# First layer norms of the last three row blocks moved to ScalarE, with statistics from summed outputs, in a fused attention and GLU kernel

## The chip, the cores and the metric

The kernel runs on one core of one Trainium2 chip. The core has a matrix engine (TensorE, PE in the profile; PEld is its weight load), a vector engine (VectorE, DVE), a scalar engine (ScalarE, ACT), a general engine (GpSimd, POOL) and a sync engine (SP), which here only issues DMAs. Each engine takes its instructions in the order in which they stand in its queue and waits on semaphores for the others. The metric is the device time of one execution in microseconds (us); less is better.

## The reference

One sequence of 2048 rows of width 576, two sublayers in fp32, each behind a layer norm without weights and with a residual:

```python
h  = x + attention(layernorm(x)) @ wo      # 32 heads of 18, each row attends to itself and
                                           # 7 earlier rows, 2 apart (sliding, dilated)
h2 = h + (sigmoid(n @ w_gate) * (n @ w_up)) @ w_down     # n = layernorm(h), width 4608

def layernorm(x, eps=1e-5):
    m, v = mean(x), var(x)
    return (x - m) / sqrt(v + eps)
```

The change concerns `layernorm(x)`, the first norm.

## The kernel before, in words

Rows are split into even and odd ones (attention steps by two rows), and each of these into two halves: four blocks of 512 rows, `BLOCKS` (0,0), (0,1), (1,0), (1,1), called 0 to 3. A block has four row tiles of 128 rows (`NS`), j = 0 to 3.

**First stage, up to about 223 us.** For each block `ln1` (line 338) takes the rows `xb`, normalises tile by tile into `xn` (`ln_j`, line 118; the last 64 columns are stored twice so that the contraction is a multiple of 128), transposes on TensorE (`tr_main`, line 137, four 128x128 transposes into a PSUM bank `mm`; `tr_rest`, line 142, one into a bank `acc`), and splits the result into a high and a low part for fp32r matmuls: `split` (line 103: ScalarE copies to the high part, VectorE subtracts for the low one) and `split_rest` (line 107, the same for the last chunk, with `th` as its output). In the profile `th` and `tl` are these parts, L104 and L105 the two halves of `split`, L108 and L109 those of `split_rest`, and `tok` is the tile behind `xn`.

`qkv` (line 377) then multiplies: for each block and each of four head groups four passes of `tok_major` (line 146) of 14 matmuls 128x432 into a bank `acc`, each evicted by ScalarE (line 384) into `ev`; after the fourth, three DMAs issued from ScalarE's queue (lines 388 and 390) write q, k and v to DRAM scratch. There are 64 such passes. `attention` (line 161) reads them back through SP (`q`, `kw`, `vw`) and is VectorE work (products, reductions, softmax, lines 182 to 219) but for one Exp on ScalarE (line 196). The generators are interleaved in the source: `norm_under` (line 424) normalises block b while passes of an earlier block are issued: block 1 under group 1 of block 0, block 2 under group 0 of block 1, block 3 under group 0 of block 2.

Four attentions of block 0 fill its output; then `front` (line 478) transposes it, projects it with `wo`, adds the residual, normalises again (`proj_j`, line 240, which calls `ln_j` too), and writes the operand to DRAM (line 505, `x<-tok` in the profile).

**Second stage.** The 4608 hidden columns of the MLP in chunks of 128, TensorE matmuls with 512 rows as the moving side (lines 609 to 616 and 723), with weights loaded and split by ScalarE and VectorE (L104 and L105, `w`, `wg`, `d`). The attention that is left, of blocks 1 to 3, and their projections run beside it. Blocks 2 and 3 share a scheme with fewer multiplications (`down_seven`, L785 to L794).

**What sets the order.** A scheduler places each engine's instructions in a fixed order when the kernel is built, from the order of the source and from priorities (`tc.high_priority`; `HI` is 400). Nothing is reordered while it runs. The first norm's priority is `2 * HI` for block 0, 0 for block 1 and `HI` for blocks 2 and 3 (line 345).

**The norm itself.** In `ln_j` VectorE takes mean and variance (two `bn_stats` over 288 columns, `bn_aggr`, an addition of eps), GpSimd raises to -1/2. For blocks 0 and 1 VectorE then subtracts and scales in one pass and copies the last 64 columns (lines 134 and 135). For blocks 2 and 3 (`on_act`) VectorE negates the mean (line 129) and ScalarE makes two passes, centring with a bias and scaling, and the small copy (lines 130 to 132).

Of the kernel before, what the change touches and what calls it, by code (L numbers as in the profile page):

```python
# [15 lines left out]
F32 = mybir.dt.float32  # L16
F32R = mybir.dt.float32r
AF = mybir.ActivationFunctionType
ALU = mybir.AluOpType
AX = mybir.AxisListType  # L20

P = 128
S = 2048
D = 576
# [6 lines left out]
NS = 4  # L31
TB = P * NS
DM = 512
DR = D - DM
DX = D + DR
# [5 lines left out]
EPS = 1e-5  # L41
# [11 lines left out]
HI = 400  # L53
# [7 lines left out]
def kernel(ctx, tc, x, wqkv, wo, wmlp, out):  # L61
    nc = tc.nc
    dve, act, pool, pe, sp = nc.vector, nc.scalar, nc.gpsimd, nc.tensor, nc.sync
# [9 lines left out]
    sm = ctx.enter_context(tc.tile_pool(name="sm", bufs=2))  # L73
# [12 lines left out]
    mhalf = cst.tile([P, 1], F32, name="mhalf")  # L86
# [16 lines left out]
    def split(hi, lo, src):  # L103
        act.activation(hi, src, AF.Copy)  # L104
        splits.append(dve.tensor_tensor(lo, src, f32(hi), ALU.subtract))  # L105

    def split_rest(t, src):
        act.activation(t, src, AF.Copy)  # L108
        dve.tensor_tensor(t[64:128], src[64:128], f32(t[64:128]), ALU.subtract)  # L109
# [5 lines left out]
                sp.dma_start(bass.AP(tensor=a.tensor, offset=a.offset,  # L115
                                     ap=[[LP * CG // 16, 16], [1, LP * CG // 16]]), zero)

    def ln_j(xj, xn, on_act):
        bs = sm.tile([P, 2, 6], F32, bufs=4, name="bs")
        mv = sm.tile([P, 2], F32, bufs=4, name="mv")  # L120
        rstd = sm.tile([P, 1], F32, bufs=4, name="rstd")
        for k in range(2):
            dve.bn_stats(bs[:, k], xj[:, k * DH2:(k + 1) * DH2])
        dve.bn_aggr(mv, bs)
        dve.tensor_scalar(rstd, mv[:, 1:2], EPS, None, ALU.add)
        pool.tensor_tensor(rstd, rstd, mhalf, ALU.pow)
        if on_act:
            nm = sm.tile([P, 1], F32, bufs=4, name="nm")
            dve.tensor_scalar(nm, mv[:, 0:1], -1.0, None, ALU.mult)
            act.activation(xn[:, :D], xj, AF.Identity, bias=nm)  # L130
            act.activation(xn[:, :D], xn[:, :D], AF.Copy, scale=rstd)
            act.activation(xn[:, D:DX], xn[:, DM:D], AF.Copy)
        else:
            dve.tensor_scalar(xn[:, :D], xj, mv[:, 0:1], rstd, ALU.subtract, ALU.mult)
            dve.tensor_copy(xn[:, D:DX], xn[:, DM:D])

    def tr_main(ps, xn):
        for c in range(4):
            pe.transpose(ps[:, c * P:(c + 1) * P], xn[:, c * P:(c + 1) * P], ident)
        return ps.rearrange("p (c n) -> p c n", c=4)  # L140

    def tr_rest(ps, xn):
        pe.transpose(ps[:, :P], xn[:, DM:DX], ident)
        return ps[:, :P]

    def tok_major(ps, n, th, tl, js, wh, wl):
        k = 0
        for c in range(4):
            for a, m in ((th, wh), (tl, wh), (th, wl)):
                pe.matmul(ps[:, :n], a[:, c, js], m[:, c], start=k == 0, stop=False)  # L150
                k += 1
        pe.matmul(ps[:, :n], th[:, 4, js], wh[:, 4], start=False, stop=False)  # L152
        return pe.matmul(ps[:, :n], th[:, 4, js], wl[:, 4], start=False, stop=True)  # L153
# [86 lines left out]
    def proj_j(bank, t, wos, th, tl, xn_tile, put, order=(0, 1)):  # L240
        oj = t[0]
        pv = tr_main(bank(), oj)
        with tc.high_priority(HI):
            split(th[:, 0:4], tl, pv)
        yield
        pv = tr_rest(bank(), oj)
        with tc.high_priority(HI):
            split_rest(th[:, 4], pv)
        yield
        for i in order:  # L250
            ps = bank()
            tok_major(ps, DH2, th, tl, slice(0, P), *wos[i])
            hs = t[1][:, i * DH2:(i + 1) * DH2]
            with tc.high_priority(HI):
                dve.tensor_tensor(hs, hs, ps[:, :DH2], ALU.add)
            yield
        xn = xn_tile()
        with tc.high_priority(HI):
            ln_j(t[1], xn, False)
        yield  # L260
        pv = tr_main(bank(), xn)
        with tc.high_priority(HI):
            put(pv, slice(0, 4))
        yield
        pv = tr_rest(bank(), xn)
        with tc.high_priority(HI):
            put(pv.unsqueeze(1), slice(4, 5))
        yield
# [18 lines left out]
    def th_tile():  # L287
        return xt.tile([P, 5, TB], F32R, tag="th", bufs=3, name="th")

    def tl_tile():  # L290
        return xt.tile([P, 4, TB], F32R, tag="tl", bufs=4, name="tl")
# [24 lines left out]
    def mm_tile():  # L316
        return psp.tile([P, 512], F32, tag="mm", bufs=3, name="mm")

    def acc_tile():
        return psp.tile([P, 512], F32, tag="acc", bufs=5, name="acc")  # L320

    def tok_tile(shape=(P, NS, DX)):
        return stk.tile(list(shape), F32, tag="tok", bufs=2, name="tok")

    def th3_tile(dt):
        return sar.tile([P, 5, TB], dt, tag="th3", name="th3")
# [4 lines left out]
    def load_x(b):  # L331
        e, hf = BLOCKS[b]
        t = sah.tile([P, NS, D], F32, bufs=2, name="h")
        for j in range(NS):
            sp.dma_start(t[:, j], xv[e, hf][:, j])
        return t

    def ln1(b, xb):
        th = th3_tile(F32R) if b == 3 else th_tile()
        tl = tl_tile()  # L340
        yield th, tl
        xn = tok_tile()
        for j in range(NS):
            js = slice(j * P, (j + 1) * P)
            pri = 2 * HI if b == 0 else HI if b > 1 else 0
            with tc.high_priority(pri):
                ln_j(xb[:, j], xn[:, j], b > 1)
            pv = tr_main(mm_tile(), xn[:, j])
            pr = tr_rest(acc_tile(), xn[:, j])
            with tc.high_priority(pri):  # L350
                split(th[:, 0:4, js], tl[:, :, js], pv)
                split_rest(th[:, 4, js], pr)
            yield
# [70 lines left out]
    def norm_under(b, xb, call, n):  # L424
        gl = ln1(b, xb)
        T.append(next(gl))
        for _ in call:
            step(ag, n)
            next(gl, END)
            step(ag, n)  # L430
        drain(gl)
# [6 lines left out]
    xb = load_x(0)  # L438
    w = [qkv_w(0, raw_w(0))]
    gl = ln1(0, xb)  # L440
    T.append(next(gl))
    run(gl, qkv(0, 0, T[0], w[0]))
    w.append(qkv_w(1))
    xb = load_x(1)
# [3 lines left out]
    xb = load_x(2)  # L448
    norm_under(2, xb, qkv(1, 0, T[1], w[0]), 1)
    xb = load_x(3)  # L450
# [27 lines left out]
    def front():  # L478
        ar = tok_tile((P, 5, TB))
        oT = th_tile(), tl_tile()  # L480
        gens = []
        for j in range(NS):
            js = slice(j * P, (j + 1) * P)

            def put(pv, cs, js=js):
                if not X:
                    X["a00"], X["a01"] = tl_tile(), th_tile()
                if cs.start == 0:
                    for t, c in ((X["a00"], 0), (X["a01"], 2)):
                        split(t[:, 0:2, js], t[:, 2:4, js], pv[:, c:c + 2])  # L490
                else:
                    split_rest(X["a01"][:, 4, js], pv[:, 0])
                act.activation(ar[:, cs, js], pv, AF.Copy)

            gens.append(proj_j(any_bank, (o[:, j], h[:, j]), wos, oT[0][:, :, js], oT[1][:, :, js],
                               lambda j=j: o[:, j], put, (1, 0)))
        k = 0
        while gens:
            with tc.high_priority(HI):
                gens = [gn for gn in gens if next(gn, END) is not END]  # L500
            k += 1
            if k == 4:
                act.dma_start(hacc[0], h)
            yield
        act.dma_start(xscr[0], ar)
# [312 lines left out]
    def proj_scr(pj, b, raw, wos, ins=None, after=None):  # L818
# [3 lines left out]
        def tile_j(t, j):  # L822
            js = slice(j * P, (j + 1) * P)

            def put(pv, cs):
                if cs.start == 0:
                    if b < 2:
                        pool.dma_start(hacc[b][:, j], t[1])
                    else:
                        rows = slice(0, 7, 6) if b == 2 else slice(2, 5, 2)  # L830
                        pool.dma_start(hsev[:, j // 2, rows, j % 2],
                                       t[1].rearrange("p (i n) -> p i n", i=2))
                act.activation(raw[:, cs, js], pv, AF.Copy)

            yield from proj_j(bg_bank, t, wos, th[:, :, js], tl[:, :, js], lambda: t[0], put, (1, 0))
# [392 lines left out]
```

## Time and profile before

| what | us |
|---|---|
| runs of the kernel | 1592.14, 1589.58, 1590.2 (median 1590.2) |
| span of the profiled execution | 1589.2 |
| TensorE busy, share of the span | 1553.3, 98% |
| VectorE | 1268.1, 80% |
| ScalarE | 869.2, 55% |
| GpSimd | 184.2, 12% |

The profile is one execution, and its span runs from the first to the last instruction. In rows of a timeline the columns are start, duration, engine, line, operation, output and inputs, shapes, count, and in square brackets how long the engine sat idle before and what released it. In rows of groups: the busy total, the mean in ns of one, and the idle time before them with its releasers. In rows of busy time by stretch: the stretch, its length, then busy time with count for PE, PEld, DVE, ACT and POOL, the granted TensorE clock (1.00 is full), the share of the DMA engines and GB/s. In rows of waits: who waited for whom, the total in us, how often, and the longest.

### The profile page before, as it was taken

What the parts mean: (1) busy time and instruction counts of PE and PEld (TensorE: products, weight loads), DVE (VectorE), ACT (ScalarE), POOL (GpSimd) and SP (SyncE); (2) the same over time, 40 slices, a digit from 0 to 9 for tenths busy, and PEclk for the clock granted to TensorE, in tenths of its full rate; (3) what the DMA queues carried; (4) which work ended last, traced back from release to release, by engine and by line L of the source; (5) the groups of instructions that cost most, each with busy time, mean ns of one, the idle gap of its engine ahead of it and who ended that gap; (6) DMA issues with size and microseconds to landing.
All of it is one profiled execution on the core that took longest, in us unless ns stands there. A gap on an engine that the chain in (4) does not pass through costs nothing.

```text
span 1589.2 us, 22383 instructions
## 1 busy us (share of the span) xinstructions
PE 1553.3 (98%) x8532; PEld 1381.6 (87%) x8532; DVE 1268.1 (80%) x1931; ACT 869.2 (55%) x1546; POOL 184.2 (12%) x230
## 2 busy tenths in 40 slices
PE   7999979999999999999989999999999999999998
PEld 6999968888888888888879988888888888888887
DVE  7999988959999999999546687876677776677755
ACT  4432234425555666656443255776677776677761
POOL 1000000011010001000101100122112112212210
PEclk9999999999999999999999999999999999999999
DMA  7664544346367565665764234899989999989983
GB/s 267 208 206 163 193 184 165 133 177 246 104 164 205 157 170 139 166 191 149 210 203 143 100 110 110 182 186 181 176 169 183 184 173 180 177 170 182 184 170 124
DMA packets 76892, 273.50 MB, mean 172 GB/s; under 512 B 8336, under 2 KB 14224, under 8 KB 75888
## 3 DMA queue, kind: packets, MB, share of 16 engines
q0 software_dynamic: 27792, 105.89, 36.3%
q1 hardware_dynamic: 41360, 146.06, 27.4%
q10 hardware_dynamic: 7632, 20.12, 3.3%
q8 instruction: 67, 1.10, 0.3%
q14 instruction: 41, 0.34, 0.1%
HBM read 145.88 MB, written 128.52 MB: 173 GB/s over the span
## 4 chain that ended last, share of the span: by engine, by line
PE 55%; issue 27%; POOL 7%; DVE 6%; DMA 4%; ACT 1%; SPq 0%; POOLq 0%; ACTq 0%; DVEq 0%
PE b L609 23%; PE dp L723 15%; POOL h L794 7%; PE acc L150 6%; PE b L616 4%; PE b L150 1%; PE bgp L150 1%; DMA wg<-in_wmlp_dram 1%; DVE pr L182 1%; DMA x<-tok 1%; DVE pr L208 1%; DVE lg L186 1%; PE acc L152 1%; DMA tail<-h 1%; PE acc L153 1%
## 5 line engine op out<-in xcount | busy, mean ns | idle before, releaser
L609 PE MATMUL b<-tl,w 128*128 128x512 f32 x1716 | 438.1, 395 | 9.1 <-ACT w L104 6.5
L609 PEld LDWEIGHTS b<-tl,w 128*128 128x128 f32 x1716 | 311.7, 189 | 66.5 <-ACT w L104 7.7
L609 PE MATMUL b<-th,w 128*128 128x512 f32 x1368 | 352.8, 393 | 0.4 <-DVE s L698 0.3
L609 PEld LDWEIGHTS b<-th,w 128*128 128x128 f32 x1368 | 249.8, 188 | 46.7 <-DVE s L698 0.7
L104 ACT ACTIVATE w<-wg 128x640 fp32r<-128x640 f32 (+2 forms) x197 | 117.0, 598 | 125.2 <-PE b L616 59.8
L791 ACT ACTIVATE ev<-dp 128x576 f32<-128x576 f32 x224 | 145.0, 647 | 61.8 <-PE dp L785 58.2
L616 PE MATMUL b<-th,w 128*128 128x512 f32 x572 | 177.0, 391 | 0.0
L794 POOL DMA_DIRECT2D h<-ev x128 | 110.2, 862 | 456.8 <-ACT ev L791 440.5
L105 DVE TENSOR_TENSOR w<-wg,w 128x640 fp32r<-128x640 f32 (+2 forms) x197 | 126.8, 649 | 38.7 <-ACT w L104 38.3
L150 PE MATMUL acc<-qw,th 128*128 128x432 f32 x512 | 155.7, 365 | 1.2 <-DVE th L109 0.9
L105 DVE TENSOR_TENSOR w<-tw,w 128x512 fp32r<-128x512 f32 x116 | 79.6, 687 | 81.1 <-ACT w L104 80.2
L616 PEld LDWEIGHTS b<-th,w 128*128 128x128 f32 x572 | 107.7, 188 | 23.1
L723 PE MATMUL dp<-d,h0h 128*128 128x288 f32 x640 | 119.0, 296 | 1.7 <-DVE tail L733 1.7
L723 PE MATMUL dp<-d,h1h 128*128 128x288 f32 x640 | 120.0, 297 | 0.0
L723 PEld LDWEIGHTS dp<-d,h0h 128*128 128x128 f32 x640 | 99.4, 189 | 5.5 <-DVE tail L733 2.0
L150 PEld LDWEIGHTS acc<-qw,th 128*128 128x128 f32 x512 | 97.2, 190 | 6.5 <-DVE th L109 1.1
L723 PEld LDWEIGHTS dp<-d,h1h 128*128 128x128 f32 x640 | 99.5, 190 | 2.9
L731 ACT ACTIVATE stage<-dp 128x576 f32<-128x576 f32 x96 | 61.7, 646 | 62.4 <-PE dp L723 62.3
L104 ACT ACTIVATE w<-tw 128x512 fp32r<-128x512 f32 x116 | 72.8, 628 | 41.3 <-PE b L609 40.9
L150 PE MATMUL acc<-qw,tl 128*128 128x432 f32 x256 | 92.8, 362 | 0.0
L384 ACT ACTIVATE ev<-acc 128x432 f32<-128x432 f32 x64 | 33.9, 531 | 104.4 <-PE acc L153 97.7
L182 DVE TENSOR_TENSOR pr<-kw,q 128x2304 f32<-128x2304 f32 x32 | 81.7, 2552 | 2.8 <-DMA kw<-k 2.6
(278 smaller groups left out, 2899.8 us busy)
## 6 DMA issues: line engine op xcount, KB each, us to landing
h<-ev POOLq DMA_DIRECT2D x96, 576.0 KB, 7.2
wg<-in_wmlp_dram SPq DMA_DIRECT2D x49, 928.0 KB, 5.2
h<-stage POOLq DMA_DIRECT2D x24, 1152.0 KB, 10.6
wg<-in_wmlp_dram SPq DMA_DIRECT2D x36, 640.0 KB, 4.1
kw<-k SPq DMA_DIRECT2D x16, 792.0 KB, 4.4
vw<-v SPq DMA_DIRECT2D x16, 792.0 KB, 5.5
wd<-in_wmlp_dram SPq DMA_DIRECT2D x18, 576.0 KB, 7.2
h<-ev POOLq DMA_DIRECT2D x32, 288.0 KB, 6.8
```

Of the source, the lines that this page charges most:

```text
L104: act.activation(hi, src, AF.Copy)
L105: splits.append(dve.tensor_tensor(lo, src, f32(hi), ALU.subtract))
L150: pe.matmul(ps[:, :n], a[:, c, js], m[:, c], start=k == 0, stop=False)
L152: pe.matmul(ps[:, :n], th[:, 4, js], wh[:, 4], start=False, stop=False)
L182: dve.tensor_tensor(pr, both(kw, u), q[:, us].unsqueeze(2).broadcast_to([P, 2, W, CG]), ALU.mult)
L384: act.activation(ev[:, :, j], ps[:, :NQ].rearrange("p (t c) -> p t c", t=3), AF.Copy)
L609: pe.matmul(ps, wt[:, a, k0 + c], xx[:, m + c], start=first and k == 0, stop=k == 5, skip_group_check=True)
L616: pe.matmul(ps, wt[:, a, k0], xx[:, 4], start=False, stop=a == 1, skip_group_check=True)
L723: pe.matmul(ps[:, i, :DH2], a[:, js], d[:, m, i * DH2:(i + 1) * DH2], start=k == 0, stop=k == n)
L731: act.activation(hv, ps, AF.Copy)
L791: act.activation(hs[:, k % 2], ps[:, :, :DH2], AF.Copy)
L794: pool.dma_start(hsev[:, u, k0:k + 1], hs[:, :k + 1 - k0], accum_op=ALU.add, max_dma_last_dim=8 * D)
```

## The change

`ln_j` loses its `on_act` branch and stays for block 0 and for the second norms. Blocks 1, 2 and 3 get two new functions. `ln_stats` makes three ScalarE passes over a tile: a copy scaled by -1/576 whose summed output is the negative mean (what it writes to `xn` is overwritten by the next pass), the centring, and a square scaled by 576^-0.5 whose summed output is the variance; it writes its squares into `xj`, the loaded rows. GpSimd adds eps and raises to -1/2. `ln_scale` makes the scaling and the small copy, both on ScalarE. In `ln1` the statistics of tile j+1 are asked for before the scaling of tile j. Priorities stay as they were.

```diff
-    def ln_j(xj, xn, on_act):
+    def ln_j(xj, xn):
...
-        if on_act:
-            nm = sm.tile([P, 1], F32, bufs=4, name="nm")
-            dve.tensor_scalar(nm, mv[:, 0:1], -1.0, None, ALU.mult)
-            act.activation(xn[:, :D], xj, AF.Identity, bias=nm)
-            act.activation(xn[:, :D], xn[:, :D], AF.Copy, scale=rstd)
-            act.activation(xn[:, D:DX], xn[:, DM:D], AF.Copy)
-        else:
-            dve.tensor_scalar(xn[:, :D], xj, mv[:, 0:1], rstd, ALU.subtract, ALU.mult)
-            dve.tensor_copy(xn[:, D:DX], xn[:, DM:D])
+        dve.tensor_scalar(xn[:, :D], xj, mv[:, 0:1], rstd, ALU.subtract, ALU.mult)
+        dve.tensor_copy(xn[:, D:DX], xn[:, DM:D])
+
+    def ln_stats(xj, xn):
+        mv = sm.tile([P, 2], F32, bufs=4, name="mv")
+        nm, var = mv[:, 0:1], mv[:, 1:2]
+        rstd = sm.tile([P, 1], F32, bufs=4, name="rstd")
+        act.activation(xn[:, :D], xj, AF.Copy, scale=-1.0 / D, accum_out=nm)
+        act.activation(xn[:, :D], xj, AF.Identity, bias=nm)
+        act.activation(xj, xn[:, :D], AF.Square, scale=D ** -0.5, accum_out=var)
+        pool.tensor_scalar(rstd, var, EPS, None, ALU.add)
+        pool.tensor_tensor(rstd, rstd, mhalf, ALU.pow)
+        return rstd
+
+    def ln_scale(rstd, xn):
+        act.activation(xn[:, :D], xn[:, :D], AF.Copy, scale=rstd)
+        act.activation(xn[:, D:DX], xn[:, DM:D], AF.Copy)
...
     def ln1(b, xb):
...
+        pri = 2 * HI if b == 0 else HI if b > 1 else 0
+        rstd = []
+
+        def stats(n):
+            with tc.high_priority(pri):
+                for j in range(len(rstd), n):
+                    rstd.append(ln_stats(xb[:, j], xn[:, j]))
+
         for j in range(NS):
             js = slice(j * P, (j + 1) * P)
-            pri = 2 * HI if b == 0 else HI if b > 1 else 0
+            if b:
+                stats(min(j + 2, NS))
             with tc.high_priority(pri):
-                ln_j(xb[:, j], xn[:, j], b > 1)
+                if b:
+                    ln_scale(rstd[j], xn[:, j])
+                else:
+                    ln_j(xb[:, j], xn[:, j])
```

More of the change, by code (lines that the diff above doesn't have):

```diff
@@ L258, in proj_j @@
         with tc.high_priority(HI):
-            ln_j(t[1], xn, False)
+            ln_j(t[1], xn)
         yield
```

## The prediction

> **What bounds the kernel now.** I read the page first, then busy time by stretch.
>
> ```profile
> PE 1553.3 (98%) x8532; PEld 1381.6 (87%) x8532; DVE 1268.1 (80%) x1931; ACT 869.2 (55%) x1546; POOL 184.2 (12%) x230
> ...
> 13.00:60.00 47.00, 45.85 (x248) 42.57 (x247) 39.81 (x103) 27.75 (x64) 6.47 (x12) 1.00 0.74 252
> 70.00:184.00 114.00, 114.00 (x582) 108.96 (x581) 109.28 (x94) 31.25 (x65) 0.91 (x1) 1.00 0.55 191
> 236.00:246.00 10.00, 7.46 (x17) 5.57 (x18) 8.66 (x12) 3.10 (x6) 0.00 (x0) 0.50 0.17 44
> 320.00:323.00 3.00, 3.00 (x18) 2.90 (x17) 1.05 (x2) 1.20 (x2) 0.00 (x0) 0.67 1.08 410
> 323.00:326.00 3.00, 3.00 (x17) 2.53 (x16) 1.69 (x3) 0.76 (x2) 0.00 (x0) 0.76 0.94 387
> ```
>
> TensorE has 98% of the span. In the attention stage, where the change lies, it is busy 45.85 of 47 us and then 114 of 114; VectorE is nearly as full (109.28 of 114), but TensorE waits for it hardly at all. So what VectorE is spared is worth only the waits below, and whatever makes TensorE late in 13 to 60 us is kept to the end. ScalarE looks free, 27.75 of 47. The waits that could be won:
>
> ```profile
> 44.92 0.47 PE L150 MATMUL acc<-qw,th 128*128 128x432 f32 x1 [0.86 <-DVE th L109]
> ...
> PE b L609 <- DVE s L629: 2.5, 1, 2.5
> PE mm L150 <- DVE tl L105: 1.3, 1, 1.3
> PE mm L139 <- DVE tok L134: 0.5, 1, 0.5
> ...
> 319.78 0.66 PE L139 MATMUL b<-ident,oj 128*128 128x128 f32 x4 [2.40 <-DMA oj<-o]
> ```
>
> **What the change takes off VectorE.** The groups of VectorE in 13 to 60 us:
>
> ```profile
> L123 DVE BATCH_NORM_STATS2 bs<-h 128x6 f32<-128x288 f32 x24 | 9.7, 438 | 0.1
> L134 DVE TENSOR_SCALAR tok<-h,mv,rstd 128x576 f32<-128x576 f32 x6 | 3.4, 575 | 1.1 <-POOL rstd L126 1.1
> L124 DVE BATCH_NORM_AGGREGATE mv<-bs 128x2 f32<-128x12 f32 x12 | 2.0, 189 | 0.0
> L125 DVE TENSOR_SCALAR rstd<-mv 128x1 f32<-128x1 f32 x12 | 1.5, 144 | 0.0
> L135 DVE COPY tok<-tok 128x64 f32<-128x64 f32 x7 | 1.3, 184 | 0.0
> L129 DVE TENSOR_SCALAR nm<-mv 128x1 f32<-128x1 f32 x8 | 1.0, 144 | 0.0
> ```
>
> Twelve tiles lose two bn_stats, an aggregate and an addition: 12 x (2 x 0.438 + 0.189 + 0.144) = 14.5 us. Block 1's four lose scaling and copy, 4 x 0.759 = 3.0; the other eight their L129, 1.2. Together 18.7 us.
>
> **What it puts on ScalarE.** The same stretch, ScalarE's groups, and one 128x576 copy with a constant scale:
>
> ```profile
> L104 ACT ACTIVATE th<-mm 128x512 fp32r<-128x512 f32 x12 | 7.2, 601 | 0.1
> L384 ACT ACTIVATE ev<-acc 128x432 f32<-128x432 f32 x13 | 6.9, 530 | 17.9 <-PE acc L153 13.8 <-DMA q<-ev 2.2 <-DMA h<-in_x_dram 2.0
> L131 ACT ACTIVATE tok<-tok,rstd 128x576 f32<-128x576 f32 x8 | 6.0, 773 | 0.9 <-POOL rstd L126 0.9
> L130 ACT ACTIVATE tok<-h,nm 128x576 f32<-128x576 f32 x8 | 5.9, 772 | 0.0
> L108 ACT ACTIVATE th<-acc 128x128 fp32r<-128x128 f32 x12 | 3.3, 278 | 0.0
> L132 ACT ACTIVATE tok<-tok 128x64 f32<-128x64 f32 x8 | 1.8, 252 | 0.0
> ...
> L104 ACT ACTIVATE d<-wg 128x576 fp32r<-128x576 f32 x50 | 33.4, 676 | 17.1 <-DMA x<-tok 8.7 <-PE dp L723 8.2
> ```
>
> Sum pass and square take 0.676 each, centring 0.772, scaling 0.773, the small copy 0.252. A tile of blocks 2 and 3 gains 2 x 0.676, one of block 1 all five: 8 x 1.35 + 4 x 3.15 = 23.4 us, against 17.9 + 0.9 us of waits in the stretch, part of them the queue's own DMA issues:
>
> ```profile
> 17.44 0.53 ACT L384 ACTIVATE ev<-acc 128x432 f32<-128x432 f32 x1 [4.42 <-PE acc L153]
> 19.96 1.01 ACT L104 ACTIVATE qw<-ws 128x432 fp32r<-128x432 f32 x2
> 28.18 0.34 ACTq L388 DMA_DIRECT2D q<-ev  x1
> 29.04 0.46 ACTq L390 DMA_DIRECT2D v<-ev  x1
> 30.78 1.44 ACT L130 ACTIVATE tok<-h,nm 128x576 f32<-128x576 f32 x2
> ...
> 36.75 0.60 PE L139 MATMUL mm<-ident,tok 128*128 128x128 f32 x4
> 40.05 0.60 PE L139 MATMUL mm<-ident,tok 128*128 128x128 f32 x4
> 40.51 0.44 PE L150 MATMUL acc<-qw,th 128*128 128x432 f32 x1
> 61.29 0.36 PE L153 MATMUL acc<-qw,th 128*128 128x432 f32 x1
> ...
> 35.95 2.56 DVE L182 TENSOR_TENSOR pr<-kw,q 128x2304 f32<-128x2304 f32 x1 [2.58 <-DMA kw<-k]
> ...
> L126 POOL TENSOR_TENSOR rstd<-rstd,mhalf x32: 549/560/1037, 5.3 to 913.8; 128x1 f32<-128x1 f32 x32
> ```
>
> Three issues hold the queue 1.3 us (28.18 to 29.50). Two passes in a row take 1.44, not 1.54: a successor that waits for nothing starts 0.10 early. TensorE needs a tile every 3.30 us (36.75 to 40.05). ScalarE's work for one is five passes, split (0.601 + 0.278), eviction (0.530) and a share of the issues (0.33), less overlaps of 0.8: 4.1 us. Twelve tiles at 0.8 us too many are 9.6 us late: a first estimate.
>
> **The queue walked.** TensorE's order of projection passes and transposes hardly changes. The changed ScalarE order puts block 2's first three tiles ahead of block 1's last two, which TensorE needs first. From 20.46, where the second split of the pair at 19.96 starts in the old trace (there is room for what comes earlier: ScalarE idled 4.42 us before 17.44), up to the scaling of block 1's tile 3 stand: 13 sum and square passes (8.8), 7 centrings (5.4), 7 scalings (5.4), 6 small copies (1.5), 7 evictions (3.7), 3 + 4 splits (2.9), one weight split (0.6): 28.3 us, less 4.3 of overlap, plus two groups of issues, 2.6, and 0.7 of waits for GpSimd and TensorE: done at 47.8. The small copy follows at 49.3, since a scaling in between waits some 1.3 us for GpSimd's two operations (the power's 0.56 each, and two hand-overs). TensorE transposed this tile at 40.05 and began the next pass at 40.51; now it begins at 49.5, 9.0 us late. Tile 2 is late too (39.6 against 36.75); that is in it.
>
> Next in the queue is the first attention's Exp. VectorE reaches it at 51.7: its kw is written 0.9 us later, its product starts at 36.9 (35.95 now), and with it 14.7 us of queue: two products and two reductions of 2.55, six splits (3.0) and the softmax's first three steps (1.5). After Exp (52.1) come 32 ScalarE instructions, 18.3 us less 3.2 of overlap plus 1.5 of waits, before block 1's last small split: 68.7. It is late in the queue, but the last two matmuls of a block 1 pass need it, after VectorE's half behind one attention product (70.4 at the earliest). Everything on TensorE stands behind them. Block 2's second pass then ends at 73.2; now it ends at 61.5 (the 61.29 row). **Lateness 11.7 us**; the 0.86 us wait is inside it. Later ScalarE has 31.25 of 114 us to do and TensorE no slack.
>
> Unknown prices. The summed output may cost nothing (0) or a small operation for each (0.252, L132's row): of the 24 some 20 lie on the walk, 0 to +5.0; I take +2.5, as nothing in the trace shows one. The Trainium skill, "VectorE: DVE Perf Modes", section "Two Vector instructions with no wait between them", counts an operation with accumulator output as two instructions; that is said of VectorE, no run here shows it, and on ScalarE with L132's price the sum would be 2.5 us more. The clock: after the 2.40 us wait at 319.78 it was 0.67 and 0.76 for 3 us each, which loses 3 x 0.33 + 3 x 0.24 = 1.7 us; after 9 us of near idleness 0.50 to 246. The last stall, about 3 us, may cost 0 to 1.7, taken +1.0; after the earlier ones ScalarE is the bound and hides it. The Trainium skill, "TensorE: Matmul & The Clock Gate", Part 1, gives an idle window of about 3.4 us for the slow state; here 2.40 us sufficed, so the trace disagrees; by the rule this term would be 0.
>
> GpSimd gains twelve additions of one column, priced like its power, and has nothing else queued there. SP loads block 3's rows only when ScalarE has finished block 1 (41 us), 10 us before they are read. The second product of raw weights waits likewise and is needed after 100 us.
>
> **The hand-over to the MLP.**
>
> ```profile
> 221.19 0.33 ACTq L505 DMA_DIRECT2D x<-tok  x1
> 222.95 1.56 PE L609 MATMUL b<-tl,wf 128*128 128x512 f32 x6
> 223.15 0.53 ACT L384 ACTIVATE ev<-acc 128x432 f32<-128x432 f32 x1 [1.99 <-PE acc L153]
> 232.36 0.68 ACT L104 ACTIVATE d<-wg 128x576 fp32r<-128x576 f32 x1 [8.68 <-DMA x<-tok]
> 233.06 1.28 ACT L653 ACT_TABLE_LOAD   x1
> ```
>
> The x write lands 11.2 us after its issue and frees ScalarE, which TensorE waits for. Now it is issued 1.8 us before TensorE's last projection ends; in the changed order it stands behind the last eviction, 0.7 us after: +2.5. An Exp with its table load (1.28 + 0.42) comes ahead of the first weight split: +1.7. VectorE no longer does 5 us of attention ahead of the product s, so that 2.5 us wait goes: -2.5. Sum +1.7; bounds -2.5 (the write lands sooner) and +4.2. The waits for VectorE at the front (1.3 + 0.5 us) may go: 0 to -1.8, taken -1.0. The wait at 319.78 hangs on the last attention of block 1, which VectorE now reaches earlier: 0 to -4.1 with its clock loss, taken -2.0.
>
> **Sum**: 11.7 + 2.5 + 1.0 + 1.7 - 1.0 - 2.0 = +13.9 on a span of 1589.2, 1603.1; the median of the runs, 1590.2, is 1.0 above the span, so **1604**. Ends: 11.7 - 2.5 - 1.8 - 4.1 = +3.3, and 11.7 + 5.0 + 1.7 + 4.2 = +22.6.
>
> **Rivals.**
> - ScalarE becomes the bound, as walked: 1604, own range 1596 to 1611. For it: the counts in the queue. Chance 0.68.
> - The same, with dear summed outputs and colder clocks, +22: 1612. For it: nothing hides either once ScalarE is the bound. Against: no row shows a second instruction. 0.17.
> - Faster: the passes fit into ScalarE's waits and VectorE's relief pays. It gets back the 0.86 us wait, 1.8 at the front, 2.5 at the hand-over and 2.0 of the 4.1: about -7.2, 1583. It decides at block 1's tile 2: if its scaling is done by 36.7, this holds. Against: 4.1 us of ScalarE work per 3.30. 0.07.
> - The stall is half as long (+5.9) and the gains of the third case without the 0.86 (-6.3) cancel it: 1590, the change only moves work. For it: ScalarE's waits in the stretch (18.8 us) nearly cover the passes added; what then decides is the order alone. Against: the order is written out in its queue. 0.08.
>
> **How the numbers follow.** Faster by over 0.2% (3.2 us, about what a measurement tells from no change): the third, plus a sliver of the fourth: 0.08. Within: most of the fourth, 0.06. Slower: 0.86. The range 1594 to 1613 leaves out the faster case and both tails.
>
> **What would show it.** Right: TensorE's first waits of 2 us or more before 70 us, released by ScalarE's scaling or small copy (block 1's tiles 2 and 3); ScalarE busy over 45 of 47 us in 13 to 60; the pass that ended at 61.5 ending at 72 to 77; VectorE idle ahead of the output projection. Wrong: that pass ending before 64, TensorE above 45 of 47, or a hand-over shorter than 12 us from the last projection to the first weight split (222.95 to 235 now).

## The result, and the profile after

The changed kernel is slower, as forecast: 1602.5 us median of 4 runs (1601.9 to 1603.6) against 1590.6 for the kernel before, ratio 1.0074, 95% interval 1.0060 to 1.0087. The profiled execution has a span of 1600.2 us, 11.0 above that of before. The page and the busy time by stretch:

```profile
PE 1556.3 (97%) x8532; PEld 1384.1 (86%) x8532; DVE 1256.0 (78%) x1867; ACT 890.4 (56%) x1606; POOL 191.6 (12%) x242
...
13.00:60.00 47.00, 38.78 (x189) 35.45 (x188) 30.58 (x40) 39.86 (x99) 9.64 (x19) 0.89 0.65 223
60.00:75.00 15.00, 10.94 (x58) 9.91 (x57) 11.11 (x15) 9.62 (x26) 5.92 (x6) 0.93 0.41 134
```

Over the whole run little moves: ScalarE is busy 21 us more, VectorE 12 us less. In 13 to 60 us TensorE falls from 45.85 to 38.78 us, ScalarE rises from 27.75 to 39.86, and the granted clock falls from 1.00 to 0.89. TensorE's timeline shows where:

```profile
38.83 1.11 PE L147 MATMUL mm<-ident,tok 128*128 128x128 f32 x4 [3.02 <-ACT tok L142]
48.28 0.66 PE L147 MATMUL mm<-ident,tok 128*128 128x128 f32 x4 [4.48 <-ACT tok L142]
49.60 0.48 PE L151 MATMUL acc<-ident,tok 128*128 128x128 f32 x1 [0.66 <-ACT tok L143]
66.02 0.46 PE L158 MATMUL acc<-qw,th 128*128 128x432 f32 x1 [0.54 <-ACT ev L404]
73.20 0.73 PE L158 MATMUL acc<-qw,th 128*128 128x432 f32 x1 [3.52 <-ACT ev L404]
77.60 0.36 PE L161 MATMUL acc<-qw,th 128*128 128x432 f32 x1
```

The first two waits are for the scalings (L142) of block 1's tiles 2 and 3, the third for its small copy (L143). The last row ends the pass whose last matmul was at 61.29: it is 16.3 us late. TensorE waits 12.2 us here, against 0.86 (at 44.92) and 0.26 (at 55.33) before, so 11.1 of the 16.3 are waits. The others are a slow clock behind the waits:

```profile
38.80:42.00 3.20, 3.17 (x11) 2.93 (x12) 3.11 (x4) 2.31 (x6) 1.67 (x6) 0.50 0.22 27
...
48.20:52.00 3.80, 3.06 (x11) 2.67 (x12) 3.12 (x8) 2.69 (x9) 0.40 (x1) 0.59 0.98 363
52.00:56.00 4.00, 4.00 (x15) 3.62 (x15) 3.93 (x4) 3.23 (x8) 1.20 (x2) 0.54 0.51 192
...
73.20:78.00 4.80, 4.79 (x18) 4.46 (x19) 4.67 (x5) 1.14 (x3) 0.00 (x0) 0.69 0.37 141
```

By the two stretches above, an estimate of what this loses is 47 x 0.11 + 15 x 0.07 = 6.2 us, each stretch times the share of the clock that was not granted. 11.1 + 6.2, less the 1.1 us by which TensorE came earlier into this part (the pass that ended with the matmul at 29.96 now ends with that at 28.84), is 16.2.

The lateness stays 16.4 us up to the first product of the split MLP weights (239.34, before 222.95). Then the hand-over gives 6.7 back. Its timeline on ScalarE, TensorE and GpSimd:

```profile
232.81 0.56 POOL L585 DMA_DIRECT2D wg<-in_wmlp_dram  x1
239.34 1.55 PE L629 MATMUL b<-tl,wf 128*128 128x512 f32 x6
239.68 0.33 ACTq L525 DMA_DIRECT2D x<-tok  x1
245.08 0.69 ACT L104 ACTIVATE d<-wg 128x576 fp32r<-128x576 f32 x1 [5.01 <-DMA x<-tok]
249.31 0.72 ACT L104 ACTIVATE w<-wg 128x640 fp32r<-128x640 f32 x1
250.08 3.16 PE L629 MATMUL b<-tl,w 128*128 128x512 f32 x6 [4.21 <-ACT w L104]
263.10 1.54 PE L629 MATMUL b<-tl,w 128*128 128x512 f32 x6
```

and of the kernel before:

```profile
224.78 0.57 POOL L565 DMA_DIRECT2D wg<-in_wmlp_dram  x1
236.03 1.22 PE L609 MATMUL b<-tl,w 128*128 128x512 f32 x2 [6.52 <-ACT w L104]
239.76 1.19 PE L609 MATMUL b<-tl,w 128*128 128x512 f32 x2 [2.50 <-DVE s L629]
253.43 1.55 PE L609 MATMUL b<-tl,w 128*128 128x512 f32 x6
```

The last row of each is the same place in the program, the product behind the twelfth down-projection matmul. From the first split-weight product to it took 30.5 us (222.95 to 253.43) and now takes 23.8: lateness 9.7. By the end it is 11.0; of these 1.3 us 0.8 is a wait for `oj` that grew from 2.4 to 3.2. What became shorter in the hand-over: the write of x lands 5.4 us after its issue instead of 11.1, and the 2.5 us wait for `s` is gone.

### The profile page after: what moved, and what is told of

It is laid out like the page before. It is cut to its first block, busy times and chain, and to the rows that moved or that the text cites. A ratio compares the mean times of both kernels' runs of the same rounds, so it can differ in the third digit from the quotient of the medians.

```text
span 1600.2 us, 22381 instructions
## 1 busy us (share of the span) xinstructions
PE 1556.3 (97%) x8532; PEld 1384.1 (86%) x8532; DVE 1256.0 (78%) x1867; ACT 890.4 (56%) x1606; POOL 191.6 (12%) x242
## 4 chain that ended last, share of the span: by engine, by line
PE 83%; DVE 9%; DMA 4%; ACT 2%; issue 1%; POOL 1%; SPq 0%; DVEq 0%; ACTq 0%; POOLq 0%
PE b L629 40%; PE dp L743 14%; PE dp L805 11%; PE b L636 7%; PE acc L158 6%; DMA wg<-in_wmlp_dram 2%; DVE lg L194 1%; PE b L158 1%; PE bgp L158 1%; DVE pr L190 1%; DVE pr L216 1%; DVE w L105 1%; DMA tail<-h 1%; PE acc L161 1%; PE acc L160 1%
## 5 line engine op out<-in xcount | busy, mean ns | idle before, releaser
L104 ACT ACTIVATE w<-wg 128x640 fp32r<-128x640 f32 (+2 forms) x197 | 117.1, 597 | 124.8 <-PE b L636 58.5
L104 ACT ACTIVATE w<-tw 128x512 fp32r<-128x512 f32 x116 | 72.8, 628 | 41.0 <-PE b L629 40.6
L404 ACT ACTIVATE ev<-acc 128x432 f32<-128x432 f32 x64 | 33.9, 530 | 97.3 <-PE acc L161 91.9
```

The costliest lines, as they stand in the source:

```text
L404: act.activation(ev[:, :, j], ps[:, :NQ].rearrange("p (t c) -> p t c", t=3), AF.Copy)
```

## The experiments

Theory A: ScalarE's queue has more passes than TensorE's pace allows, whatever their order. O: the order in which they are asked for makes the lateness. Hand-over and lateness below are read in one profiled execution each; single executions differ by a few us (the profiled one of `e8_b2_only` took 1593.2 us, 1.9 below its median; `h4_after_sp`, edited behind that point, comes to it 2.8 us later than the changed kernel), so verdicts rest on the medians and on which waits are there. The kernel before had a median of 1589.9 to 1590.9 beside them; each ratio is to its own. "Late" is the start of the first split-weight product against 222.95, "hand-over" the stretch just defined, "x" the time from issue to landing of the write of x.

| kernel | median us | ratio to before, 95% | late | hand-over | x |
|---|---|---|---|---|---|
| before | 1590.6 | 1 | 0 | 30.5 | 11.1 |
| after | 1602.5 | 1.0060 to 1.0087 | 16.4 | 23.8 | 5.4 |
| e1_b1_vector | 1604.8 | 1.0068 to 1.0100 | 18.4 | 24.2 | 5.3 |
| e2_b1_only | 1594.3 | 1.0008 to 1.0029 | 8.7 | 24.1 | 5.1 |
| e3_no_sums | 1588.5 | 0.9975 to 0.9995 | 2.3 | 23.9 | 5.3 |
| e4_prio | 1606.5 | 1.0079 to 1.0109 | 18.3 | 26.7 | 10.4 |
| e6_eps_dve | 1597.1 | 1.0027 to 1.0054 | 13.5 | 23.9 | 5.3 |
| e7_b3_only | 1589.4 | 0.9983 to 1.0000 | -0.7 | 29.6 | 10.9 |
| e8_b2_only | 1595.1 | 1.0019 to 1.0038 | 10.0 | 24.0 | 5.2 |
| h3_before_act | 1585.4 | 0.9957 to 0.9980 | -0.6 | 27.6 | 11.0 |
| h4_after_sp | 1603.3 | 1.0057 to 1.0095 | 19.2 | 22.7 | 4.5 |
| c1_b3_act | 1586.5 | 0.9966 to 0.9984 | -1.0 | 27.3 | 11.5 |

**The added passes left out.** In all three blocks the sum and square passes go, and the norms use constants for mean and variance; centring, scaling, small copy and GpSimd's two operations stay.

```diff
-        act.activation(xn[:, :D], xj, AF.Copy, scale=-1.0 / D, accum_out=nm)
-        act.activation(xn[:, :D], xj, AF.Identity, bias=nm)
-        act.activation(xj, xn[:, :D], AF.Square, scale=D ** -0.5, accum_out=var)
-        pool.tensor_scalar(rstd, var, EPS, None, ALU.add)
+        act.activation(xn[:, :D], xj, AF.Identity, bias=mhalf)
+        pool.tensor_scalar(rstd, mask[:, 0, 7:8], EPS, None, ALU.add)
```

> The sum pass and the square pass are left out in blocks 1 to 3 (the norm uses constants for mean and variance), everything else of the change stays, with VectorE relieved as much. Theory A: ScalarE adds only block 1's 4 x 1.8 = 7 us, TensorE is at most 2 us late, and what remains is the worth of VectorE's relief: 1580 to 1588. Rival B (GpSimd, the loads, or the queue's order and not the passes): above 1594.

1588.5 us, 0.5 above what A gave and far below B: these passes, with the waits that hang on them, make the loss. Among these waits are those for GpSimd, whose two operations no longer depend on a ScalarE pass here. TensorE's waits for the scalings are gone, a wait of 2.5 us for VectorE (L109, at 55.64) is left and with it a lateness of 2.3 us, and the hand-over's gain remains.

**Block 1 back on VectorE**, blocks 2 and 3 as changed.

```diff
-            if b:
+            if b > 1:
```

> Block 1's norm goes back to VectorE; blocks 2 and 3 keep the five ScalarE passes. Theory A (the amount of ScalarE work ahead of TensorE's transposes is the bound): ScalarE's additions fall from 12 tiles to 8 x 1.5 us = 12 us, which its waits nearly hold; TensorE is 0 to 4 us late at the pass that ended at 61.5 before, and the earlier hand-over to the MLP (7 us in the changed kernel) is kept in part: 1585 to 1593. Rival B (the loads of block 3 or GpSimd's two operations, which stay for 8 tiles, make it late): above 1596.

A missed: 1604.8 us, no better than the change. The time is in B's range, but neither of B's causes is there: up to 80 us ScalarE waits for GpSimd 1.4 us in all, and none of TensorE's waits ends with a load of block 3. The timelines of this kernel, TensorE, VectorE and ScalarE:

```profile
44.09 0.73 PE L158 MATMUL acc<-qw,th 128*128 128x432 f32 x1 [5.32 <-ACT th L104]
49.99 1.11 PE L147 MATMUL mm<-ident,tok 128*128 128x128 f32 x4 [5.17 <-DVE tl L105]
...
38.89 2.56 DVE L190 TENSOR_TENSOR pr<-kw,q 128x2304 f32<-128x2304 f32 x1 [10.40 <-DMA kw<-k]
46.66 2.55 DVE L194 TENSOR_REDUCE lg<-pr 128x128 f32<-128x2304 f32 x1
49.25 0.69 DVE L105 TENSOR_TENSOR tl<-mm,th 128x512 fp32r<-128x512 f32 x1
...
42.63 0.26 ACT L143 ACTIVATE tok<-tok 128x64 f32<-128x64 f32 x1 [2.53 <-DMA v<-zero]
```

Another mechanism stands here, in the second of the two waits. VectorE's queue, rid of the statistics of blocks 2 and 3, has the first attention's two products and two reductions (10.2 us) straight behind block 1's scalings, ahead of the low halves of the splits. They wait for `kw` until 38.89, and the low half that TensorE needs runs at 49.25 although ScalarE's half was done at 44. The first wait ends with ScalarE's split (L104, at 43.46): it stands in ScalarE's queue behind passes of block 2 and behind 2.5 us in which ScalarE stood at its DMA issues until the zeros of v (`v<-zero`) had landed. So block 1's passes are not the only cause.

**Block 1 alone on passes**, blocks 2 and 3 as before (their `on_act` branch put back, `if b == 1` for the passes).

> Only block 1 has the summed ScalarE passes; blocks 2 and 3 are as before (statistics by VectorE, two passes and the small copy by ScalarE). Theory A: additions of 4 x 3.3 = 13 us, most of them in 13 to 50 us; TensorE 2 to 8 us late, no more than half of the changed kernel's 16: 1588 to 1598. Rival O (it is the order, block 2's passes ahead of block 1's last tiles, not the amount): the order stays as it is in the changed kernel, so most of the loss stays: 1597 to 1603.

1594.3 us, as A has it and under O's 1597. One wait of TensorE, for the scaling of a tile of block 1, replaces the two:

```profile
45.89 1.12 PE L154 MATMUL mm<-ident,tok 128*128 128x128 f32 x4 [7.12 <-ACT tok L149]
```

It is 8.7 us late, a little over the 8 that A allowed, and the hand-over is 6.4 us shorter.

**The order alone.** All passes stay; block 1's are asked for ahead of block 2's.

```diff
-        pri = 2 * HI if b == 0 else HI if b > 1 else 0
+        pri = 2 * HI if b == 0 else HI + 100 if b == 1 else HI
```

> Block 1's passes get a priority above those of blocks 2 and 3 and stand ahead of them; the amount of work is that of the changed kernel. Rival O (order): TensorE is no longer late for block 1 and catches up: 1583 to 1592. Theory A (amount): the wait moves to blocks 2 and 3, the pass that ended at 61.5 ends at 69 to 76 and the time is 1593 to 1602.

Both missed the time: 1606.5 us. TensorE's waits up to 60 us shrink to 3.0. As A said, a wait moves to a later tile's scaling (65.20), and the pass that ended at 61.5 ends at 70.4. But more of the loss reappears on the other side of the stage. The timelines on TensorE, ScalarE and VectorE:

```profile
65.20 0.93 PE L147 MATMUL mm<-ident,tok 128*128 128x128 f32 x4 [3.05 <-ACT tok L142]
...
197.83 0.44 PE L147 MATMUL mm<-ident,tok 128*128 128x128 f32 x2 [2.48 <-DVE tok L227]
203.00 0.87 PE L151 MATMUL acc<-ident,tok 128*128 128x128 f32 x3 [4.52 <-DVE tok L429]
...
77.76 0.40 ACT L204 ACTIVATE lg<-lg 128x256 f32<-128x256 f32 x1
...
80.32 2.55 DVE L216 TENSOR_TENSOR pr<-vw,lg 128x2304 f32<-128x2304 f32 x1
```

The first attention's Exp now stands behind the passes, at 77.76 instead of 50.41 in the changed kernel, so VectorE's weighted sum starts at 80.32 instead of 52.96. VectorE does not make this up, and the output projection waits 7.0 us for it at 200 us. O falls for this order: with the same work it only chose who waits. Other orders were not run.

**GpSimd out of half of its part.** The addition of eps goes to VectorE, the power stays.

```diff
-        pool.tensor_scalar(rstd, var, EPS, None, ALU.add)
+        dve.tensor_scalar(rstd, var, EPS, None, ALU.add)
```

> The changed kernel, with EPS added by VectorE instead of GpSimd; GpSimd keeps only the power. Theory G (GpSimd's two operations, stretched beside VectorE's attention products, are part of what makes the scalings late): ScalarE's waits for rstd, 6.5 us between 13 and 75 us, fall to 4 or less, the first product of the split MLP weights starts 1 to 4 us before the changed kernel's 239.3, time 1598 to 1602 us. Rival Q (the addition waits in VectorE's queue behind a product instead): these waits stay at 6 us or more, time 1602 to 1607 us.

1597.1 us, the direction of G and 0.9 below its range; its interval lies wholly below that of the change. ScalarE's waits in 13 to 75 us, the changed kernel and this one:

```profile
ACT tok L142 <- POOL rstd L138: 6.5, 6, 2.2
```

```profile
ACT tok L142 <- POOL rstd L138: 1.7, 4, 0.7
```

TensorE's 3.52 us wait at 73.20 is gone, while those for the scalings of block 1's tiles stay (3.03 and 5.23 us). The chain of the 3.52 us wait in the changed kernel, by the timelines of VectorE, GpSimd and ScalarE:

```profile
68.33 2.56 DVE L190 TENSOR_TENSOR pr<-kw,q 128x2304 f32<-128x2304 f32 x1
68.84 2.12 POOL L137 TENSOR_SCALAR rstd<-mv 128x1 f32<-128x1 f32 x1 [2.43 <-ACT h L136]
71.65 0.78 ACT L142 ACTIVATE tok<-tok,rstd 128x576 f32<-128x576 f32 x1 [2.24 <-POOL rstd L138]
72.33 0.26 ACT L108 ACTIVATE th<-acc 128x128 fp32r<-128x128 f32 x1
72.62 0.29 DVE L109 TENSOR_TENSOR th<-acc,th 64x128 fp32r<-64x128 f32 x1 [0.69 <-ACT th L108]
72.63 0.52 ACT L404 ACTIVATE ev<-acc 128x432 f32<-128x432 f32 x1
```

An addition on one column lasts until VectorE's attention product ends; the scaling waits for it; behind the scaling in ScalarE's queue stand block 1's last small split (L108) and an eviction (L404), which depend on neither. VectorE adds its half of the split at 72.62, the eviction, which TensorE's row names, ends at 73.15, and TensorE goes on at 73.20.

**Block 3 alone, block 2 alone** (passes with summed output for that block, the others as before).

> Passes with summed output for the first norm of block 3 alone; blocks 1 and 2 as in the kernel before. Theory A (the lateness comes from the amount of passes on ScalarE's queue ahead of the evictions and splits that TensorE waits for, and block 3's have the latest need): start of the split MLP weights' products 223 to 226 us, time 1588 to 1594 us. Theory O (the order in which the passes are asked for makes it, whatever the amount): 229 us or later, time 1596 us or more.

> Passes with summed output for the first norm of block 2 alone; blocks 1 and 3 as in the kernel before. Theory A (amount of passes on ScalarE ahead of what TensorE waits for): with four passes with summed output in the place of the statistics on VectorE, fewer than block 1's, a lateness at the start of the split MLP weights' products of 0 to 5 us (223 to 228 us), time 1585 to 1594 us, the lower half of it if VectorE's attention is then one product further when that start comes, as its queue has it here. Rival V (taking the statistics out of VectorE's queue lets attention products of block 0 stand ahead of the low parts of the splits, whichever block they come from): a lateness over 6 us, time 1592 us or more.

Block 3's passes cost nothing (1589.4 us, no lateness): ScalarE is busy 31.75 of 47 us in 13 to 60, TensorE 46.25. Block 2's cost about as much as block 1's, and V's marks came (10.0 us late, 1595.1 us). Its trace has two waits, as with block 1 back on VectorE. The first, 5.2 us, ends with ScalarE's split, which stands behind block 2's passes and was held up 2.4 us at the issue of the write of v; this one is not V's. The second, 4.8 us, the profile puts down to an addition on VectorE which ended last; with it, just ahead of 50.08, ended the low half of a split, and both stand behind the products, which is V's mechanism:

```profile
44.55 0.73 PE L165 MATMUL acc<-qw,th 128*128 128x432 f32 x1 [5.23 <-ACT th L104]
50.08 1.12 PE L154 MATMUL mm<-ident,tok 128*128 128x128 f32 x4 [4.80 <-DVE rstd L125]
```

The time, 1595.1, is above the 1594 that A allowed.

**The hand-over.** First the kernel before, with the MLP's second weight load issued by ScalarE behind the write of x (`xw` holds this write's instruction); then the changed kernel, with this load issued by SyncE.

```diff
-        wg2 = load_gu(1, pool)
+        with tc.issue_after(getattr(xw[0], "ins", xw[0])):
+            wg2 = load_gu(1, act)
```

> The kernel before, with one line moved: the MLP's second weight load (928 KB) is issued by ScalarE right behind the write of x instead of by GpSimd. Theory H (the loads that move beside the write of x set when it lands, and its landing frees ScalarE for the MLP's weights): the write takes at most 9 us instead of 11.1, the hand-over (start of the first product with the first split weights to the start of the first with the second ones) at most 12 us instead of 13.1, time 1585 to 1589.5 us. Rival R (the write's own size and the order on ScalarE set it): the write 10.5 us or more, time 1589.5 to 1592 us.

```diff
-        wg2 = load_gu(1, pool)
+        wg2 = load_gu(1, sp)
```

> The changed kernel, with the MLP's second weight load issued by SyncE instead of GpSimd, so that it starts at about 236 us, some 3 us ahead of the write of x, instead of at 232.8. Theory H: the write takes 7 us or more instead of 5.4, the hand-over 12 us or more instead of 10.7, time 1603.5 to 1607 us. Rival R: the write stays below 5.8 us, time 1601.5 to 1603.5 us.

The first has H's time, 1585.4 us, and not its mechanism: the write still takes 11.0 us, and the hand-over as H defined it grew to 14.3 us. What changed is VectorE's order, here the first three rows, of the edited kernel, against those of before:

```profile
228.14 2.56 DVE L182 TENSOR_TENSOR pr<-kw,q 128x2304 f32<-128x2304 f32 x1
232.30 0.76 DVE L105 TENSOR_TENSOR d<-wg,d 128x576 fp32r<-128x576 f32 x1 [1.60 <-ACT d L104]
235.55 0.69 DVE L631 TENSOR_TENSOR s<-s,b 128x512 f32<-128x512 f32 x1
```

```profile
233.08 0.76 DVE L105 TENSOR_TENSOR d<-wg,d 128x576 fp32r<-128x576 f32 x1 [4.34 <-ACT d L104]
233.75 2.55 DVE L182 TENSOR_TENSOR pr<-kw,q 128x2304 f32<-128x2304 f32 x1
238.92 0.69 DVE L629 TENSOR_TENSOR s<-s,b 128x512 f32<-128x512 f32 x1
```

A logit product that stood behind the split of `d`, which waits for the write of x, now stands ahead of it, in time in which VectorE was idle, and `s` comes 3.4 us earlier, the low halves of the weights behind it. At the end of the hand-over this kernel is 3.5 us ahead, and the wait for `oj`, 2.4 us before, is 0.8. The second edit was no test of what it was meant for: SyncE issued the load at 226.6 us, not 236, so it had landed ahead of the write, which took 4.5 us. Its time, 1603.3, is that of the change, as R has it.

Over all twelve kernels the hand-over sorts itself by two things. Product behind the split and x at 11: 29.6 and 30.5 us (before, e7). Product ahead, x at 10.4 to 11.5: 26.7 to 27.6 (e4, h3, c1). Product ahead, x at 5.1 to 5.4: 23.8 to 24.2; with x at 4.5 (h4): 22.7. So the product and the landing are worth about 3 us each, by single executions; in the kernels with the early landing the reduction behind the product stands ahead of the split too, and its share was not separated. In the five kernels with the slow write GpSimd's or ScalarE's 928 KB load was issued 2.3 to 4.4 us behind it, in the others ahead of it. SyncE's own 928 KB load sorts them the same way: it was issued 0.8 to 1.4 us ahead of the slow writes and 3.5 us ahead of the others. Which of the two loads makes the write slow, or whether it is either, was not isolated.

**Both gains together**: `e7_b3_only` with the first hand-over edit.

> Passes with summed output for block 3 alone and the MLP's second weight load issued by ScalarE behind the write of x. If the two gains add, the write of x takes 10 us or more as in both, the wait for s at the first MLP products is gone, and the time is 1583 to 1586 us; if the gain of the moved load hangs on when VectorE reaches its last logit product, and that is as early here already, 1586 to 1590 us.

1586.5 us: the signs of the first case came (the write takes 11.5 us, the 2.5 us wait for `s` is gone), but the time lies 0.5 above its range, in the second one. So the two gains do not show as a sum. `h3_before_act`, whose 1585.4 is the best time found, is the kernel before with one load moved, without any of the passes; the intervals of the two overlap.

## Why the prediction held, point by point

The runs together: without the added passes the loss is gone. Alone, block 1's passes cost 3.4 us and block 2's 5.2, against the kernel before beside them, and block 3's nothing; GpSimd's additions are 5.4 us of the loss. With block 1 or block 2 changed differently from the others (`e1_b1_vector`, `e8_b2_only`), VectorE's fixed order is a second cause, and a gain at the hand-over hides part of the loss.

- **ScalarE bounds the stretch, first at block 1's tiles 2 and 3**: held. They were transposed at 38.83 and 48.28, where the walk had the scalings done at 39.6 and 47.8; the next pass was to start at 49.5, and the small copy's transpose started at 49.60. But ScalarE was busy 39.86 of 47 us there, not over 45: among its waits are 2.3 us for GpSimd and 3.1 us for TensorE's passes.
- **Lateness 11.7 + 2.5 + 1.0 = 15.2 at the end of block 2's second pass**: measured 16.3, the end being at 78.0, just past the 72 to 77 named. (The row at 61.29 ends at 61.65, not 61.5, so the walk's own 11.7 is 11.55.) The walk had 3.5 us of ScalarE's waits in all, for GpSimd and others; those for GpSimd alone were 6.5.
- **Summed outputs +2.5**: a separate instruction each, 0.19 us long and 0.09 from start to start, 24 x 0.09 = 2.2. The rows of ScalarE's timeline:

```profile
26.04 0.67 ACT L134 ACTIVATE tok<-h 128x576 f32<-128x576 f32 x1
26.61 0.19 ACT L134 ACTIVATION_READ_ACCUMULATOR tok<-h 128x1 f32 x1
26.70 0.67 ACT L134 ACTIVATE tok<-h 128x576 f32<-128x576 f32 x1
```

  The Trainium skill, "VectorE: DVE Perf Modes", section "Two Vector instructions with no wait between them", has such an operation as two instructions on VectorE; this trace shows it for ScalarE.
- **Clock +1.0, with the earlier stalls hidden because ScalarE is the bound**: mis-sized. The slow clock accounts for 6.2 of the 16.3 us. How much of it the next wait would have swallowed was not separated.
- **VectorE's relief of 18.7 us**: it was 12.1. The 18.7 add up durations; taking off 0.1 us for a successor that starts early, as the walk did for ScalarE, gives an estimate of 12.3 for 64 instructions fewer. No term of the sum used it.
- **Waits at the front -1.0**: nothing came back between 77 and 239 us (16.3, then 16.4), although VectorE stood idle 11.3 us there (up to 166.33, waiting for `kw`), as foreseen.
- **Hand-over +1.7**: the step that failed; it was -6.7, outside the bounds of -2.5 and +4.2, and from the last projection to the first weight split it took 10.0 us (239.34 to 249.31), a sign of being wrong by the prediction's own words. The sum held the write of x at 11.2 us and only moved its issue; it landed after 5.4. GpSimd's load was then ahead of it and not behind it; that this is the reason was not isolated. The other terms came about as priced: the issue moved 2.1 us (2.5), the Exp with its table load stood ahead of the weight split, and the 2.5 us for `s` went. These and the landing give -4.4; the 2.3 us that are left were not separated, and fit the low halves of the weights coming sooner with `s`, which no term had.
- **`oj` -2.0**: it was +0.8, a wait of 3.2 us instead of 2.4.
- **Sum +13.9**: measured +11.0 by the spans and +11.9 by the medians. The lateness was 2.2 larger than the 14.2 summed up to the front, the hand-over 8.4 better, the rest 3.3 worse. That the total came within 1.5 us of the forecast (1602.5, 1604) is in part luck: these misses partly cancel. With the hand-over as priced the time would have been about 1611 (1602.5 + 8.4, an estimate), at the end of the first rival's own range.
- **Rivals**: ScalarE as the bound held. Of the dear case the second instruction and the colder clock came, without adding up to +22. The faster case fell where it was to be decided: tile 2's scaling ended at 38.78, not by 36.7. A lateness that the order alone makes did not survive `e4_prio`. The case in which the gains cancel the stall did not come: a gain of its size was there, 6.7 us against 6.3, but all of it at the hand-over, with a stall of 16.4 instead of 5.9.

## What to carry to other kernels

A queue that looks idle on average may still have no room where work is added: compare its work for one tile with the pace at which the next engine needs tiles, and with the waits that fall between. Work taken off an engine moves what stands behind it in its fixed order, which may be a long instruction that waits for a load; look at what comes first then. A stall is priced with the slow clock behind it (here some 6 us beside 11 us of waits), and part of its lateness can be given back where a later stage was waiting for a transfer, as here at the hand-over.

## What was not expected of the hardware

- GpSimd's addition on one column lasted 0.21 to 0.22 us where no product of two operands ran beside it, but 2.12 and 2.40 beside VectorE's 2.56 us product of two SBUF operands, ending with it. The Trainium skill, "SBUF — State Buffer", section "Who interferes with whom", says that a VectorE instruction with two SBUF inputs contends with a GpSimd instruction that reads SBUF, one blocking the other for its whole length; the trace agrees.
- Waits of 3.02 and 4.48 us on TensorE were each followed by a granted clock of 0.50 to 0.59 for 3 to 8 us.
- The same write of 1280 KB took 4.5 to 5.4 us in seven kernels and 10.4 to 11.5 in the five others; why is open.
